# Splitting the decay-gate chain by columns, turning the first q and k in fp32, and more filler matmuls, in a fused attention and SwiGLU kernel

## The chip, the cores and the metric

The kernel runs on one core of one Trainium2 chip. The metric is the time of one execution in microseconds (us) on the device. Runs of one kernel mostly agree within a per cent. Some runs fall in a slower state; they are marked slow and are left out of every comparison below. Where two kernels are compared, they ran on the same chip in alternating rounds. The ratio given is the mean time of one kernel's fast runs over the mean of the other's fast runs in the same rounds, with a 95% interval, so it is not quite the ratio of the medians that are quoted beside it.

A traced run also has a span, from its first to its last instruction. The span is about 1.7 us shorter than the time of the same run.

Names: PE is TensorE's matmul pipe, PEld its loading of the stationary operand, DVE is VectorE, ACT ScalarE, POOL GpSimd, SP SyncE. "SPq" is the DMA issue queue of SyncE.

## The reference

```python
# q, k, v: (8, 8, 576, 64), f: (8, 8, 576), fp32; w_gate, w_val: (512, 1536); w_out: (1536, 512)
scores = q @ k^T / sqrt(64)
cum    = cumsum(log(clip(f, 1e-4, 1)))               # along the sequence
attn   = softmax(causal(scores + cum_i - cum_j))     # per batch and head
x      = (attn @ v) as 4608 tokens x 512
out    = (silu(x @ w_gate) * (x @ w_val)) @ w_out
```

The decay `cum_i - cum_j` is not added to the scores. It is written as four extra rows (a high, a middle and a low part of `cum` in bf16, against rows of ones) under the 64 rows of q and of k. So a score matmul contracts over 68 rows, and the first score needs q, k and these rows.

## The kernel before

All instructions come from a planner. Each piece of work is registered as an `op` with its engine, what it comes after, the buffers it takes and a priority. At build time the planner simulates the engines with guessed durations and emits each operation when it becomes the best one for its engine. Each engine then runs its instructions strictly in that order. What the planner decides is therefore fixed in the program: if one operand comes late on the chip, everything behind it on that engine waits.

The gate chain makes the decay rows of all 64 heads at once, and four ScalarE-issued transfers put those of batches 0 and 1 (`hh` to `QK`) where the score matmuls read them:

```python
o_clip = op(("DVE", ...), ... lf = min(max(lf, 1e-4), 1) ...)
o_ln   = op(("ACT", 0.6), lambda e: nc.scalar.activation(lf, lf, AF.Ln), after=[o_clip], key=-9)
o_scan = op(("DVE", 1.4), ... cum = cumsum(lf), 576 columns at once ..., key=-9)
o_hi   = op(("DVE", 0.7), ... dec[1] = -8 * cum ...)
o_up   = op(("ACT", 0.6), ... dec[0] = 8 * cum ...)
# ... o_r1, o_mid, o_lo: the rest of cum after the bf16 rounding, twice
def row(e, r):
    nc.scalar.dma_start(
        out=QK[D + r : D + r + 1, : FIRST * FB, :, :S].rearrange("o b (j w) s -> o (b j) w s", w=2),
        in_=dec[r][: FIRST * H].rearrange("h w s -> h (w s)"),
    )
```

The queries and keys of a pair of heads are loaded in fp32 as they lie, cast to bf16, turned by six bf16 transposes on TensorE and copied out of PSUM into `QK`:

```python
o1 = op(("SP", SPi), ld_qk, p, nm, bn, ...)                 # load
o2 = op(copier(QT * 2 * D, False), cast_qk, bn, bb, ...)    # fp32 -> bf16, any engine
o3 = op(("PE", mm(*[P] * QT)), turn, bb, bt, ...)           # six transposes
# straighten: two copies out of PSUM, ACT or DVE
```

The weights of the gate products are loaded in four pieces each of `w_gate` and `w_val`, 384 KB a transfer, issued by GpSimd not before a planned time:

```python
w_ready[nm, c] = op(("POOL", SW), weights, t, src, c, key=-3, dma=2.6, ready=W_AT[c] + (nm == "v"))
W_AT = [15.0, 19.0, 36.0, 42.0]
```

While TensorE has nothing to do in the simulated plan, before 22 us, the planner emits filler matmuls. They multiply the identity by itself into an unused bank and only keep TensorE active:

```python
if e == "PE" and idle and idle[0] <= t < idle[1] and self.free["f"]:
    idle[2](self.free["f"][-1])        # dummy(bank)
    busy[e] = t + idle[3]
...
span = plan.run((2.0, IDLE_TO, dummy, 0.2))     # IDLE_TO = 22.0
```

The parts left out are the attention (`score`, `expo`, `mask`, `weigh`, `flip`), the feed-forward part (`gate`, `tanh`, `silu`, `times`, `project`) and the later batches, which the change leaves alone.

The softmax here doesn't subtract the row's maximum and nothing guards it: scores larger than these inputs give would overflow.

## Time and profile before

| | before |
|---|---|
| time, median (four runs) | 410.09 us (409.21 to 515.33, the longest slow) |
| span of the traced run | 407.9 us |
| TensorE busy | 95% of the span |
| first score matmul | 20.97 us |
| first gate matmul | 39.07 us |
| granted clock at half | 14.6 to 35.1 us |

(The prediction read 14.2 to 35.05 us for this stretch; the clock record of the trace has 14.62 to 35.10. The 14.08 us from the first score to 35.05 and their half, 7.04, are kept below: they change by less than 0.1 us.)

The page of the profile cuts the span into 40 equal slices of 10.2 us. A digit is the busy share of a slice in tenths (9 means 90% or more); for PEclk it is the clock that the throttle granted, in tenths of full speed. The DMA row is the mean busy share of the 16 DMA engines. This is the page of the kernel before:

```profile
PE   7399999999999999999999999999999999999995
...
PEclk9757999999999999999999999999999999999999
DMA  9998999249752986979799787975211002002002
```

From the fifth slice on, TensorE is full to the end and its clock is granted. Only the first three or four slices, the head, have anything to give. The timeline of TensorE shows the head closer. A row has the start, the length, the engine and line, the operation with its output and inputs, how many instructions it groups, and in brackets how long TensorE had been idle before it and what ended that. L729 are fillers, L383 transposes, L491 scores, L623 gate matmuls. This is the kernel before, from 11 to 40 us:

```profile
start us, us, engine line op out<-in xcount [idle before <-releaser]
...
13.80 0.60 PE L729 MATMUL ps<-ident 128*128 128x256 bf16 x4 [2.46 <-ACT QK L290]
...
15.16 0.85 PE L383 MATMUL ps<-ident,BF 128*128 128x128 bf16 x6
20.97 0.80 PE L491 MATMUL ps<-QK 68*128 68x256 bf16 x4 [4.96 <-DMA QK<-hh]
...
39.07 0.60 PE L623 MATMUL ps<-xT,wg 128*128 128x256 bf16 x4
```

TensorE stood still for 2.46 us and again for 4.96 us, until the decay rows (`hh`) had landed. The busy times by stretch (microseconds busy and instructions of each engine, then clock, DMA share and GB/s) show what this did to the clock. Kernel before:

```profile
core 0: us, PE busy (x) PEld busy (x) DVE busy (x) ACT busy (x) POOL busy (x), PEclk, DMA share, GB/s
14.00:21.00 7.00, 2.04 (x20) 1.58 (x19) 3.87 (x6) 2.55 (x4) 2.43 (x3) 0.54 1.23 156
21.00:35.00 14.00, 14.00 (x129) 11.46 (x130) 7.07 (x19) 11.12 (x26) 9.14 (x26) 0.50 1.09 207
35.00:50.00 15.00, 13.63 (x181) 11.25 (x180) 12.38 (x27) 13.01 (x30) 10.19 (x26) 1.00 1.08 196
```

From 21 to 35 us TensorE is busy all the time at clock 0.50. In between the DMA share stays above 1: it sums the packets that are under way on each engine, from several queues, so it can exceed 1. The chain of waits (start, length, what) of the kernel before says what the first score hung on:

```profile
10.87 0.76 DVE hh L344
...
13.11 7.72 DMA QK<-hh
...
20.97 0.80 PE ps L491 x4
```

The step of the gate chain in this view (L344, the rounding of the middle part) ends at 11.6 us, the last subtraction (L345) at 12.4 us. The four row transfers were issued from 9.7 to 13.1 us. The last of them took until 20.8 us to land, and the other three had landed only at 18.3 to 18.9 us.

### The profile page before, as it was taken

The page shows a single profiled execution, that of the slowest core. Times are in us where ns is not written, and L with a number is a line of the kernel's source. Part 1 is how long each engine was busy: PE and PEld are TensorE (multiplying, and loading weights), DVE is VectorE, ACT ScalarE, POOL GpSimd, SP SyncE. Part 2 cuts the span into 40 slices and gives each one's busy share as a digit, 9 for nine tenths or more (in the row PEclk, how much of TensorE's full clock was granted, in tenths as well). Part 3 has the DMA queues.
Part 4 walks back from the last instruction along what each step waited for, and adds up shares of the span by engine and source line. Part 5 has one row for each costly group of instructions (what it writes and reads, how often), then busy time and mean ns, then how long its engine had stood idle before and what let it go on. Part 6 is the DMA issues. An engine that isn't in the chain of part 4 may idle for free.

```text
span 407.9 us, 8397 instructions
## 1 busy us (share of the span) xinstructions
PE 388.7 (95%) x3110; PEld 228.8 (56%) x3155; DVE 236.6 (58%) x453; ACT 222.2 (54%) x450; POOL 127.5 (31%) x353
## 2 busy tenths in 40 slices
PE   7399999999999999999999999999999999999995
PEld 4277778745655555555555555556665444444542
DVE  7756888745784287237651775177624861770850
ACT  6378997436853646365655664566677322322321
POOL 7565754504441423234333431433333000000000
PEclk9757999999999999999999999999999999999999
DMA  9998999249752986979799787975211002002002
GB/s 202 200 233 159 208 219 201 53 137 205 144 112 67 196 188 106 140 130 199 107 172 234 139 132 115 233 123 96 55 53 51 2 0 104 2 0 104 1 21 71
DMA packets 103673, 50.11 MB, mean 123 GB/s; under 512 B 87696, under 2 KB 98448, under 8 KB 103312
## 3 DMA queue, kind: packets, MB, share of 16 engines
q1 hardware_dynamic: 97056, 38.65, 46.9%
q0 software_dynamic: 6304, 10.62, 15.8%
q8 instruction: 25, 0.41, 0.4%
q10 hardware_dynamic: 272, 0.30, 0.4%
q14 instruction: 16, 0.13, 0.1%
HBM read 38.34 MB, written 15.78 MB: 133 GB/s over the span
## 4 chain that ended last, share of the span: by engine, by line
PE 90%; DMA 3%; DVE 2%; ACT 2%; issue 1%; DVEq 0%; ACTq 0%
PE ps L623 45%; PE ps L638 23%; PE ps L491 12%; PE ps L522 7%; PE ps L546 2%; DMA QK<-hh 2%; PE ps L383 2%; DVE QK L292 1%; DMA xT<-in_q_dram 1%; ACT QK L290 1%; DVE hh L337 0%; ACT L336 0%; DVE hh L342 0%; ACT PT L499 0%; DVE hh L339 0%
## 5 line engine op out<-in xcount | busy, mean ns | idle before, releaser
L623 PE MATMUL ps<-xT,wv 128*128 128x512 bf16 (+3 forms) x467 | 111.0, 357 | 0.6
L623 PE MATMUL ps<-xT,wg 128*128 128x512 bf16 (+3 forms) x465 | 110.7, 357 | 0.9 <-issue 0.2
L627 ACT ACTIVATE th<-ps 128x512 f32<-128x512 f32 (+3 forms) x120 | 66.6, 555 | 74.7 <-PE ps L623 71.3
L638 PE MATMUL ps<-wo,hh 128*128 128x512 bf16 (+1 forms) x427 | 104.5, 379 | 0.8
L631 DVE SCALAR_TENSOR_TENSOR th<-th,ps 128x512 f32<-128x512 f32 (+3 forms) x120 | 75.5, 629 | 50.4 <-ACT th L627 49.8
L499 ACT ACTIVATE PT<-ps 128x512 bf16<-128x512 f32 (+2 forms) x192 | 92.6, 509 | 19.8 <-PE ps L491 14.5
L634 DVE TENSOR_TENSOR hh<-th,ps 128x512 bf16<-128x512 f32 (+3 forms) x120 | 76.1, 634 | 12.8 <-PE ps L623 0.9
L491 PE MATMUL ps<-QK 68*128 68x320 bf16 (+4 forms) x448 | 76.9, 273 | 5.5 <-DMA QK<-hh 5.0
L508 POOL TENSOR_SCALAR_AFFINE_SELECT PT<-PT 128x128 bf16<-128x128 bf16 (+1 forms) x192 | 53.1, 278 | 90.4 <-ACT PT L499 83.5
L623 PEld LDWEIGHTS <-wg 128*128 128x128 bf16 x480 | 44.8, 97 | 37.3 <-issue 0.4
L638 PEld LDWEIGHTS <-hh 128*128 128x128 bf16 (+1 forms) x444 | 41.7, 98 | 40.7 <-issue 1.2
L623 PEld LDWEIGHTS <-wv 128*128 128x128 bf16 x480 | 44.9, 97 | 34.7
L508 POOL TENSOR_SCALAR_AFFINE_SELECT PTa<-PTa 128x256 bf16<-128x256 bf16 x64 | 26.1, 409 | 87.8 <-ACT PTa L499 86.5
L642 ACT ACTIVATE ot<-ps 128x512 f32<-128x512 f32 (+1 forms) x37 | 22.1, 597 | 49.6 <-PE ps L638 47.9
L522 PEld LDWEIGHTS <-PT 128*128 128x128 bf16 x768 | 39.8, 99 | 15.0 <-POOL PT L508 0.8
L529 DVE RECIPROCAL rc<-ps 128x5 f32<-128x5 f32 (+2 forms) x64 | 12.3, 192 | 61.9 <-PE ps L522 61.6
L522 PE MATMUL ps<-VB,PT 128*128 128x65 bf16 x768 | 47.5, 196 | 0.1
L491 PEld LDWEIGHTS <-QK 68*128 68x128 bf16 x448 | 36.4, 101 | 19.4 <-issue 6.8
L499 ACT ACTIVATE PTa<-ps 128x384 bf16<-128x384 f32 x64 | 31.2, 491 | 20.0 <-PE ps L491 19.9
L292 DVE COPY QK<-ps 64x576 bf16<-64x576 bf16 x27 | 20.2, 753 | 17.1 <-PE ps L383 15.3
L536 DVE TENSOR_TENSOR xn<-ps,rc 128x320 bf16<-128x320 f32 x56 | 27.5, 491 | 1.7
L292 POOL CAST VB<-natv 128x512 bf16<-128x512 f32 (+1 forms) x34 | 20.3, 615 | 2.7 <-DMA natv<-in_v_dram 2.7
(50 smaller groups left out, 185.8 us busy)
## 6 DMA issues: line engine op xcount, KB each, us to landing
out_dram<-ot SPq DMA_DIRECT2D x35, 256.0 KB, 2.3
natv<-in_v_dram SPq DMA_DIRECT2D x32, 256.0 KB, 7.2
xT<-in_q_dram SPq DMA_DIRECT2D x10, 288.0 KB
xT<-in_k_dram SPq DMA_DIRECT2D x10, 288.0 KB, 11.0
qk_d<-in_q_dram POOLq DMA_DIRECT2D x5, 576.0 KB, 6.2
qk_d<-in_k_dram POOLq DMA_DIRECT2D x5, 576.0 KB, 6.9
wg<-in_moe_w_gate_dram POOLq DMA_DIRECT2D x4, 384.0 KB, 8.4
wv<-in_moe_w_val_dram POOLq DMA_DIRECT2D x4, 384.0 KB, 10.8
```

The costliest lines, as they stand in the source:

```text
L292: E[e].tensor_copy(dst, src)
L491: nc.tensor.matmul(s[:, c : c + w], QK[:KR, hqk[p].i, 2 * j + 1, kt * P : (kt + 1) * P], QK[:KR, hqk[p].i, 2 * j, q0 : q0 + w], start=True ...
L499: nc.scalar.activation(place(h, i)[:, OFFS[i] : OFFS[i] + c], ps(bs)[:, :c], AF.Exp, scale=0.125)
L508: nc.gpsimd.affine_select(out=d, in_=d, pattern=pat, compare_op=ALU.is_ge, fill=0.0, base=0, channel_multiplier=-1,)
L522: nc.tensor.matmul(o[:, lo : lo + D + 1], pt[:, c : c + P], VB[hvb[b].i][:, kt, hb, : D + 1], start=first and n == 0, stop=last and n == l ...
L536: nc.vector.tensor_mul(XN[bx.i][:, qb : qb + nq, j], o, r)
L623: nc.tensor.matmul(ps(bf)[:, :n], w[:, ko, fc * P : (fc + 1) * P], xT[:, ko, t0 : t0 + n], start=(ko == 0), stop=(ko == KD - 1))
L627: nc.scalar.activation(TH[bt.i][:, :n], ps(bf)[:, :n], AF.Tanh, scale=0.5)
L631: nc.vector.scalar_tensor_tensor(out=t, in0=t, scalar=1.0, in1=ps(bf)[:, :n], op0=ALU.add, op1=ALU.mult)
L634: nc.vector.tensor_mul(HH[:, bh.i, lo : lo + n], TH[bt.i][:, :n], ps(bf)[:, :n])
L638: nc.tensor.matmul(ps(bf)[:m, :DM], HH[:, hs[fc].i, lo : lo + m], wo[:, fc, :], start=(fc == 0), stop=(fc == KF - 1))
L642: nc.scalar.activation(OT[bo.i][:m], ps(bf)[:m, :DM], AF.Copy, scale=0.5)
```

## The change

The intent is to start the attention earlier and to keep TensorE's clock up on the way:

- The chain is cut into columns 0 to 255 and 256 to 575. The first score blocks need only the first 256 columns, so four small row transfers leave early, on SyncE. The transfers of the second part follow later.
- The q and k of batch 0 are loaded in halves, turned in fp32 without a cast, and cast when they are copied out of PSUM.
- The scratch of the gate chain moves from the hidden buffer `hh` to unused columns of `xT`. So the 432 KB store of the later batches' decay can wait until 45 us.
- Filler matmuls are allowed until 40 us of the simulated plan (22 before); 95 are emitted instead of 39.
- All planned times and priorities are set anew.

```diff
-    o_scan = op(("DVE", 1.4), lambda e: nc.vector.tensor_tensor_scan(
-        out=cum, data0=lf, data1=zero, initial=0.0, op0=ALU.add, op1=ALU.add), after=[o_ln, o_zero], key=-9)
+    CUTS = (slice(0, HALF), slice(HALF, S))
+    def scan(e, c):
+        x = CUTS[c]
+        nc.vector.tensor_tensor_scan(out=cum[:, x], data0=lf[:, x], data1=zero[:, x], op0=ALU.add, op1=ALU.add,
+                                     initial=cum[:, HALF - 1 : HALF] if c else 0.0)
# ... the other steps of the chain likewise, for c in 0, 1
-        nc.scalar.dma_start(                                   # row: four transfers, ACT
+        for p0, p1, x in ((0, FB, CUTS[c]),) if c == 0 else ((0, FB, CUTS[c]), (FB, FIRST * FB, slice(0, S))):
+            E[e].dma_start(                                    # row: four first, eight second, SP
+                out=QK[D + r : D + r + 1, p0:p1, :, x]..., in_=dec[r][2 * p0 : 2 * p1, :, x])
+    def turn_x(e, p, half, xs, bt):
+        ...     nc.tensor.transpose(o, natx[half][p][:, x, h, P * y : P * y + P], ident32[:m, :m])
+    def first_queries(p):
+        for half in range(2):
+            lds = [op(("SP", SPi), ld_x, p, nm, x, half, ...) for x, nm in enumerate("qk")]
+            ...     o3 = op(("PE", ...), turn_x, p, half, xs, bt, ...)
+            ...     straighten_x on ACT or DVE, with the cast
-    queries(0, 0)
-    ...
+    for p in range(FB):
+        first_queries(p)
-    span = plan.run((2.0, IDLE_TO, dummy, 0.2))
+    span = plan.run((2.0, IDLE_TO, dummy, 0.107))
-W_AT = [15.0, 19.0, 36.0, 42.0]
+W_AT = [9.0, 14.5, 11.3, 31.6]
-IDLE_TO = 22.0
+IDLE_TO = 40.0
# ... cuts: the planner's model of DMA queues, buffers, priorities of the other loads
```

## The prediction

> **What bounds the kernel now.** TensorE. In the busy times per stretch it works 301.3 of 303.5 us from 100 us to its last matmul; from 35.05 us on it idles 4.5 us in all. The tail after it is 4.4 us. Only the head can give much. There the chain of waits shows the gate chain, row transfers QK<-hh from 13.11 to 20.83 us, and the first score matmul at 20.97. By microsecond, the granted clock is 1.00 to 14 us, 0.50 from 14.2 to 35.05, then 1.00: matmuls had stopped from 11.3 to 13.8 and 16.0 to 20.97. From 20.97 to 35.05 TensorE is fully busy at 0.50: 14.08 us for 7.04 us of work. The Trainium skill ("TensorE: Matmul & The Clock Gate", Part 1) says that an idle window of about 3.4 us halves the clock and a busy one restores it; here restoring took 14 busy us, so losing the clock costs more than the page suggests.
>
> **What the change does.**
> - The gate chain (scan 1.35, subtract 1.26, 0.75 us) is cut into 256 and 320 columns; the first row sends need only the first part. They stand behind about 2 MB of loads; 0 to 10 us moved 201 GB/s. The 432 KB decay store that competed with the rows moves to much later.
> - Batch 0: eight casts (0.55 to 0.84 us) and 48 bf16 transposes (6 in 0.50 us warm) go; 48 fp32 transposes come. Copies out of PSUM become 24 of 320 to 512 elements (estimate 0.4 to 0.65 us, from the 256- and 512-element ones here) instead of 16 of 0.65 to 0.75. Net relief of the other engines about 5 us, estimate.
> - First weights are asked for at about 9 us instead of 18.5, and gate matmuls stand much earlier in TensorE's order.
> - Fillers 39 -> 95: 62 before the first score, 33 after.
>
> **On the critical path.** First score: 62 fillers (0.22 us cold to about 8 us, 0.11 to 0.14 warm) and six groups of transposes end near 14 us; rows land at about the same time. I put it at 15.2 us (-5.8). Clock kept: -7.0. Against this: at full clock TensorE outruns ScalarE (79% busy from 21 to 35 us with TensorE at half speed) and DMA (share above 1 until 33 us): I expect 6 us idle or filler from first score to 50 us, before 1.4: +4.6. fp32 transposes after first score +1.4 (estimate). Sum -6.8; with the relieved engines -7.7.
>
> **Prediction: 402.5 us, range 396.5 to 408.5.** Chances: faster by over 2% 0.46, within 2% 0.50, slower 0.04.
>
> **Signs.** Right: first score matmul at 14 to 17 us; granted clock 1.00 from 9 us on; first gate matmul before 30 us instead of 39; last matmul about 7 us earlier; the length from 100 us on unchanged; ScalarE over 90% busy from 16 to 45 us. Wrong: clock back at 0.50 after the first score; row sends landing after 18 us; TensorE idle over 8 us between first score and 50 us, released by weights (DMA) or ScalarE.
>
> **What would make it wrong.** Slower: the attention matmuls (68 rows, 65 columns) may count as too little activity, since 14 busy us did not raise the clock; then 7 us come back. Row sends sharing with weight loads may land late, fillers run out, and the gap drops the clock. Fillers placed for a guessed timeline may delay real work. Faster: if gate matmuls fill TensorE after the first score, the gain approaches 11 us (about 399).

## The result, and the profile after

| | before | after |
|---|---|---|
| time, median (four runs each, the longest of each slow) | 410.09 us (409.21 to 515.33) | 406.67 us (406.17 to 412.7) |
| ratio of fast runs | | 0.992 [0.9896, 0.9944] |
| span of the traced run | 407.9 us | 404.4 us |
| first score matmul | 20.97 us | 14.92 us |
| first gate matmul | 39.07 us | 28.92 us |
| last matmul ends | 403.53 us | 400.46 us |
| granted clock at half | 14.6 to 35.1 us | 24.6 to 31.4 us |

The change is worth 3.4 us where 7.7 us were forecast; the time lies within the range. The page of the changed kernel:

```profile
PE   8969999999999999999999999999999999999996
...
PEclk9979999999999999999999999999999999999999
DMA  8999999047953985899699789986102002002002
```

The third slice has still lost clock. The timeline of TensorE in the changed kernel from 14 us on (L813 fillers, L580 scores, L485 fp32 transposes, L635 flips, L712 gate matmuls):

```profile
13.83 1.25 PE L813 MATMUL ps<-ident 128*128 128x256 bf16 x10
14.92 1.32 PE L580 MATMUL ps<-QK 68*128 68x256 bf16 x14
...
22.27 0.50 PE L485 MATMUL ps<-ident,xT 80*128 80x80 f32 x4 [1.95 <-DMA xT<-in_k_dram]
...
24.39 2.03 PE L580 MATMUL ps<-QK 68*128 68x192 bf16 x10 [0.99 <-DMA QK<-xT]
...
27.17 0.74 PE L485 MATMUL ps<-ident,xT 80*128 80x80 f32 x4
28.09 0.77 PE L485 MATMUL ps<-ident,xT 80*128 80x80 f32 x4 [0.17 <-DMA xT<-in_k_dram]
...
28.92 1.06 PE L712 MATMUL ps<-xT,wg 128*128 128x256 bf16 x4
```

The first score starts at 14.92 us as intended. Then TensorE waits for two things that it had not waited for before: at 22.27 us for the second half of pair 2's k, at 24.39 us for the rows of the second part. The busy times by stretch show the new loss of clock, in 25 to 30 us, and a DMA share of 1.14 to 1.37 all through. Changed kernel:

```profile
14.00:20.00 6.00, 5.77 (x75) 4.96 (x74) 2.76 (x9) 4.19 (x10) 5.56 (x13) 1.00 1.24 242
20.00:25.00 5.00, 2.07 (x25) 1.53 (x22) 1.58 (x6) 1.96 (x6) 2.85 (x5) 0.96 1.37 199
25.00:30.00 5.00, 4.80 (x26) 3.33 (x25) 1.31 (x3) 3.06 (x7) 0.82 (x3) 0.50 1.23 234
30.00:35.00 5.00, 4.93 (x44) 4.07 (x44) 2.53 (x6) 4.55 (x12) 3.81 (x13) 0.86 1.14 210
```

The chain of waits of the changed kernel at this place consists of loads alone, until the last turn at 28.09 us:

```profile
13.61 8.62 DMA xT<-in_k_dram
...
22.24 5.71 DMA xT<-in_k_dram
...
28.09 0.78 PE ps L485 x4
```

The issue queue of SyncE in the changed kernel shows how they line up. L352 are row transfers, about 0.68 us each; L473 are halves of q and k:

```profile
13.61 0.44 SPq L473 DMA_DIRECT2D xT<-in_k_dram  x1
14.14 5.88 SPq L352 DMA_DIRECT2D QK<-xT  x6
20.07 0.44 SPq L473 DMA_DIRECT2D xT<-in_q_dram  x1
22.24 0.32 SPq L473 DMA_DIRECT2D xT<-in_k_dram  x1
```

The trace also shows why one load follows from another in the chain. SyncE gives each transfer the semaphore of the eighth before it and waits until that one has landed. The k half issued at 22.24 us has the semaphore of the k half issued at 13.61, whose last landing is at 22.22 us.

Beside them GpSimd issues the six weight transfers (changed kernel, GpSimd's timeline, the first and the last of the six):

```profile
9.52 0.99 POOL L708 DMA_DIRECT2D wg<-in_moe_w_gate_dram  x1
...
15.88 0.79 POOL L708 DMA_DIRECT2D wv<-in_moe_w_val_dram  x1
```

The account, worked out from the two traces, after minus before: first score -6.05; clock -3.8 (7.04 us lost before; 3.3 after, half of the 6.56 us that TensorE was busy from 24.58 to 31.41); fillers after the first score +3.5 (33 of 0.107 us); TensorE idle from first score to 50 us +2.1 (3.4 against 1.4); more transposing after the first score +1.0; tail -0.4. The sum is -3.7 and the span's change is -3.5. Such an account adds terms as if they were independent, and the experiments show that they are not.

### The profile page after: what moved, and what is told of

It is laid out like the page before. It is cut to its first block, busy times and chain, and to the rows that moved or that the text cites. A ratio compares the mean times of both kernels' runs of the same rounds, so it can differ in the third digit from the quotient of the medians.

```text
span 404.4 us, 8602 instructions
## 1 busy us (share of the span) xinstructions
PE 394.4 (98%) x3211; PEld 232.3 (57%) x3211; DVE 230.6 (57%) x452; ACT 224.9 (56%) x457; POOL 128.9 (32%) x357
## 4 chain that ended last, share of the span: by engine, by line
PE 91%; DMA 4%; DVE 1%; POOL 1%; ACT 1%; issue 0%; SPq 0%; ACTq 0%; DVEq 0%
PE ps L712 46%; PE ps L727 24%; PE ps L580 10%; PE ps L611 7%; DMA xT<-in_k_dram 4%; PE ps L635 2%; PE ps L418 1%; DMA xT<-in_f_dram 1%; PE ps L813 0%; DVE xT L321 0%; POOL PT L380 0%; DVE QK L297 0%; POOL xT L328 0%; POOL wg L708 0%; SPq L352 0%
## 5 line engine op out<-in xcount | busy, mean ns | idle before, releaser
L712 PE MATMUL ps<-xT,wg 128*128 128x512 bf16 (+3 forms) x480 | 113.7, 359 | 0.0
L712 PE MATMUL ps<-xT,wv 128*128 128x512 bf16 (+3 forms) x480 | 113.4, 358 | 0.1
L727 PE MATMUL ps<-wo,hh 128*128 128x512 bf16 (+1 forms) x444 | 106.3, 379 | 0.0
L588 ACT ACTIVATE PT<-ps 128x384 bf16<-128x384 f32 (+2 forms) x192 | 93.0, 507 | 23.8 <-PE ps L580 14.0
L580 PE MATMUL ps<-QK 68*128 68x320 bf16 (+4 forms) x448 | 72.9, 265 | 1.1 <-DMA QK<-xT 1.0
L712 PEld LDWEIGHTS <-wv 128*128 128x128 bf16 x480 | 45.0, 98 | 35.5 <-issue 0.4
L712 PEld LDWEIGHTS <-wg 128*128 128x128 bf16 x480 | 45.1, 98 | 35.3
L611 PEld LDWEIGHTS <-PT 128*128 128x128 bf16 x768 | 38.3, 97 | 17.7 <-POOL PT L597 1.1
L611 PE MATMUL ps<-VB,PT 128*128 128x65 bf16 x768 | 45.4, 193 | 0.0
L580 PEld LDWEIGHTS <-QK 68*128 68x128 bf16 x448 | 35.1, 98 | 11.8 <-issue 1.7
L588 ACT ACTIVATE PTa<-ps 128x384 bf16<-128x384 f32 x64 | 30.7, 491 | 15.4 <-PE ps L580 15.2
L295 ACT ACTIVATE QK<-ps 64x576 bf16<-64x576 bf16 (+2 forms) x31 | 19.3, 627 | 9.9 <-DVE QK L297 8.1
L297 POOL CAST VB<-natv 128x512 bf16<-128x512 f32 (+1 forms) x38 | 23.2, 620 | 4.6 <-DMA natv<-in_v_dram 4.6
```

Of the source, the lines that this page charges most:

```text
L297: E[e].tensor_copy(dst, src)
L580: nc.tensor.matmul(s[:, c : c + w], QK[:KR, hqk[p].i, 2 * j + 1, kt * P : (kt + 1) * P], QK[:KR, hqk[p].i, 2 * j, q0 : q0 + w], start=True ...
L588: nc.scalar.activation(place(h, i)[:, OFFS[i] : OFFS[i] + c], ps(bs)[:, :c], AF.Exp, scale=0.125)
L611: nc.tensor.matmul(o[:, lo : lo + D + 1], pt[:, c : c + P], VB[hvb[b].i][:, kt, hb, : D + 1], start=first and n == 0, stop=last and n == l ...
L712: nc.tensor.matmul(ps(bf)[:, :n], w[:, ko, fc * P : (fc + 1) * P], xT[:, ko, t0 : t0 + n], start=(ko == 0), stop=(ko == KD - 1))
L727: nc.tensor.matmul(ps(bf)[:m, :DM], HH[:, hs[fc].i, lo : lo + m], wo[:, fc, :], start=(fc == 0), stop=(fc == KF - 1))
```

## The experiments

All but two of the experiments (`w_none` and `whole`) edit what the planner has emitted, its order, its fillers or the queue of a transfer, and nothing else. The planner's emissions are recorded as a list `log` of (operation, engine), with `None` for a filler and its bank; the list is edited and then emitted. By its code, a list without an edit emits the kernel it came from; no run checks this, but the trace of `w_late`, which only moves transfers, has as many instructions as that of the changed kernel (8602). `at(tag)` is the place of an operation in the list. All results were correct except where said. Medians are of six runs, the kernel before's of eleven in the same rounds. The changed kernel's own median of 406.67 us comes from other rounds, so small differences to it are read from traces, and differences of medians under about 1 us are not relied on.

Two marks are read from the traces: the first gate matmul, and the first matmul of the output projection (called first projection below), before which every one of these kernels has issued the same 192 gate matmuls. From the first projection to the last matmul the time is nearly fixed: 329.27 us in the changed kernel, 329.27 in `fill_gap`, 329.25 in `no_post_fill`, 329.26 in `w_at_20`; 327.18 in the kernel before, 327.18 in `before_fill`, 327.19 in `before_fill_store_late`. So in these traces what moves the first projection arrives at the end. Between the two kernels even this mark needs care: the changed one reaches it 5.17 us earlier (71.18 against 76.35 us), but leaves 15 score matmuls and 15 of the products with v for later, and takes 2.09 us longer from there.

Theory A, of the prediction: the clock that fell again and the fillers are the missing 4 us. Theory D: the order of SyncE's queue delays what TensorE waits for. Theory A1: the weight transfers take the DMA engines from the loads. Theory E: the head up to the first gate is bound by what the DMA engines move altogether, so that what TensorE gains there is waited away, while from the first gate on TensorE passes on any delay to the end. Rival R: the end is set elsewhere.

### Holding the clock through the gap

```diff
+ n = at(("turnx", 2, 1), 1);  log[n:n] = [(None, 1)] * 18     # before the late transposes
+ n = at(("s", 0, 1));         log[n:n] = [(None, 3)] * 9      # before the second-part scores
```

> The changed kernel with 27 fillers added where its trace shows TensorE waiting on transfers: 18 before the transposes that started at 22.27 us, 9 before the second-part scores that started at 24.39 us. Nothing else moves. Theory A (the gaps of 1.95 and 0.99 us let the clock fall at 24.8 us, and 6.4 us at half speed cost 3.2 us): the granted clock stays 1.00 after 14 us, and the time falls by about 3 us, to about 403.5 us, for the fillers stand in waits and cost nothing. Rival C (the activity of the attention matmuls is too low, whatever stands in the gaps): the clock falls to 0.50 near 25 us again and the time stays within 0.7 us of 406.6. If the fillers outlast the waits, up to 1 us is lost.

Measured: 407.1 us, ratio to before 0.9945 [0.9921, 0.9968], traced span 404.8 us. The clock stayed at 1.00 until 29.7 us (mean 0.97 from 25 to 30 us, 0.50 in the changed kernel) and was then at half for 3.41 us instead of 6.83. Nothing was gained: TensorE reached pair 3 earlier and waited for its halves instead. Timeline of TensorE with the gap filled:

```profile
27.70 0.47 PE L485 MATMUL ps<-ident,xT 80*128 80x80 f32 x4 [0.64 <-DMA xT<-in_k_dram]
...
28.15 0.60 PE L712 MATMUL ps<-xT,wg 128*128 128x256 bf16 x4
```

The first gate comes at 28.15 instead of 28.92 us. But the half-clock stretch, 29.71 to 33.12 us, now lies behind it, and the first projection comes at 71.59 instead of 71.18 us. So holding the clock up to the first gate was worth 0.77 us there: the rest of the loss lay in the shadow of these transfers. Theory A's mechanism (the gap drops the clock) held.

The run doesn't test a clock that stays full behind the first gate too, as A had expected. From the first gate to the first projection `gate_late` (below), at full clock, needs 41.42 us; the changed kernel, with 2.49 us at half clock, 42.26; this run, with 3.41 us at half clock, 43.44. An estimate from these numbers puts the first projection of a changed kernel with a full clock throughout at 28.15 + 41.42 = 69.57 us at best, 1.6 us earlier than it was. That is about half of what A expected, and no run shows it.

### Removing the fillers after the first score

```diff
+ n = at(("s", 0, 0));  log[n:] = [x for x in log[n:] if x[0] is not None]
```

> The changed kernel without the 33 fillers that stand after the first score matmul. My ledger counts 3.5 us for them. If they cost that: the 15 of them after 31 us give back 1.6 us, and the 18 before 24 us nothing, because TensorE then waits for transfers anyway: about 405 us if the clock falls no earlier. Rival (the fillers after the first score hold the clock): the clock falls before 22 us instead of at 24.8 and stays down longer, time 407 to 412 us.

Measured: 406.52 us, ratio 0.9942 [0.9917, 0.9967], traced span 404.4 us. The clock fell earlier (mean 0.71 from 20 to 25 us), and the first gate came at 29.02 us. The first projection came at 71.18 us in both. The 33 fillers neither cost nor help; their +3.5 us in the account was time in which TensorE would have waited or run at half clock (10.24 us of it here, 6.83 in the changed kernel).

### Fillers in the kernel before, without the rest of the change

```diff
+ n = ...  log[n:n] = [(None, 3)] * 23      # in the gap at 11.3 us
+ n = at(("s", 0, 0));  log[n:n] = [(None, 0)] * 46
```

> The kernel before with 69 fillers added in its two gaps (23 after 11.3 us, 46 before the first score at 20.97 us) and nothing else changed. It measures the clock term of the prediction by itself. My prediction's arithmetic: the clock stays 1.00, 7.0 us come back, and up to 4.6 us of that is lost again to ScalarE and DMA, which gives 403 to 408 us with the first score still at about 21 us. If keeping the clock is worth its full 7 us: 403. If TensorE at full clock only waits for the other engines: 408 to 410. Rival C (attention matmuls have too little activity to hold the clock): the clock falls again within 8 us of the first score, and the time is within 1.5 us of 410.

Measured: 406.25 us, ratio 0.9937 [0.991, 0.9965], traced span 403.9 us, mean clock of the whole run 1.000. The first score comes at 21.53 us, 0.56 later than before, and the first gate at 35.38 us instead of 39.07. This is the changed kernel's gain from two short lists of fillers, without the early rows and the fp32 turning. Timeline of TensorE in that kernel:

```profile
21.53 0.49 PE L491 MATMUL ps<-QK 68*128 68x256 bf16 x4 [0.96 <-DMA QK<-hh]
...
35.38 0.60 PE L623 MATMUL ps<-xT,wg 128*128 128x256 bf16 x4
```

The busy times of that kernel:

```profile
14.00:21.50 7.50, 6.56 (x65) 5.71 (x65) 4.00 (x6) 2.69 (x4) 2.44 (x4) 1.00 1.20 160
21.50:35.00 13.50, 12.33 (x190) 9.76 (x190) 10.85 (x26) 13.11 (x33) 10.43 (x30) 1.00 1.21 241
```

From 21.5 to 35 us TensorE runs at full clock, and ScalarE is busy for 13.11 of 13.50 us. The attention matmuls that ran at half clock from 21 to 35 us in the kernel before hold the full clock here, so rival C of the expectation falls. In the old order, too, the full clock is not worth the 7.04 us that half the pulses of 14.08 us amount to. From the first score to the first gate it took 18.10 us before and 13.85 here, 4.25 less. That ScalarE sets the rate then is argued from its busy share of 97% and not tested; TensorE itself counts as busy for 12.33 of the 13.50 us.

### A later start of the scores

```diff
+ n = at(("s", 0, 0));  log[n:n] = [(None, 3)] * 28
```

> The changed kernel with 28 fillers (3.0 us at full clock) added directly before the first score matmul, which then starts near 17.9 us instead of 14.9. Theory D (until 28 us TensorE waits for transfers anyway, so the early start is off the critical path): the time stays within 0.8 us of 406.6. If the early start does pay: about 409.5 us.

Measured: 407.29 us, ratio 0.9951 [0.9923, 0.9979], traced span 406.3 us. The first score started at 18.02 us instead of 14.92, the second-part scores at 24.48 instead of 24.39, the last turn at 28.39 instead of 28.09 and the first gate at 29.22 instead of 28.92. Its timeline at the first gate:

```profile
29.22 1.06 PE L712 MATMUL ps<-xT,wg 128*128 128x256 bf16 x4
```

Of 3.1 us given away, 0.3 reached the first gate, and 0.35 the first projection (71.53 us). (The traced span holds another 1.37 us of a wait at 248 us, of which more below.) So nearly 3 of the 6 us gained at the first score are off the critical path.

### Reordering SyncE's queue, with and without later weights

```diff
+ n = first second-part row transfer in log
+ log[n:n] = [k half of pair 2, q and k halves of pair 3]     # moved from later places
  # loads_first_w_late: also the gate weights c2 and c1 after mask(7, 0), at about 20 us
```

> The changed kernel with only the order of the SyncE queue changed: the second half of k of pair 2 and the second halves of q and k of pair 3 are issued before the second row sends instead of between and after them. New theory D: in the changed kernel the pair-3 halves are issued at 20.1 and 22.2 us, because each of six row sends takes about 0.7 us of the queue and a load waits for the eighth before it; they land near 28 us, and TensorE, which takes its instructions in order, cannot start the first gate matmul before that, so the six microseconds won at the first score are lost again. D expects the pair-3 halves to land before 23 us, the first gate matmul at 24 to 26 us instead of 28.9, and 403 to 405.5 us. Rival A1 (the weight transfers' share of the DMA engines sets the landing, whatever the order): the pair-3 halves land after 25 us or the row sends slip as far, and the time stays within 0.8 us of 406.6.

> The order of the run before this one, and the second and third pair of gate weights issued at about 20 us, after the eighth mask. If order and contention both matter, the halves and the rows all land by 21 us, the clock stays 1.00 and the time is 401 to 404.5 us. If contention does not matter once the order is right (D alone): equal to the run with only the order, within 0.8 us. If the late weights then hold up gate matmuls: slower than that run by 1 us or more.

Measured: 410.36 us, ratio 1.0024 [0.9988, 1.0059], for the first (its traced run is slow, so its trace is not used) and 410.57 us, 1.003 [1.0016, 1.0045], for the second, with a span of 408.8 us. In the second, the k half of pair 2 was turned at 20.87 us instead of 22.27. But the rows, now behind the loads, were late instead:

```profile
28.17 2.19 PE L580 MATMUL ps<-QK 68*128 68x192 bf16 x10 [6.16 <-DMA QK<-xT]
...
32.44 1.06 PE L712 MATMUL ps<-xT,wg 128*128 128x256 bf16 x4
```

TensorE waited 6.16 us for them. The order in the queue decides who is late, but a better order than the planner's was not found here. Theory D explains which wait ends last, not that there is one.

### Later weights: four of six, all six, and spread

```diff
  # w_late: weights c2, c1 moved after mask(7, 0)
  # w_at_20: all six
+ late = [log.pop(at(("w", nm, c))) for c in (0, 2, 1) for nm in "gv"]
+ n = at(("mask", 7, 0)) + 1;  log[n:n] = late
  # w_mid: c0 before mask(0, 0), c2 after mask(4, 0), c1 after mask(7, 0)
```

> The changed kernel with the second and third pair of gate-weight transfers issued after the eighth mask (about 20 us) instead of at 12.6 to 15.9 us; nothing else moves. Theory A1 (the second halves of k and the second rows landed late, at 22.2 and 24.4 us, because the weight queue took the larger share of the DMA engines): they land at least 2 us earlier, the gap before 22.27 us shrinks below 0.7 us, the clock stays 1.00 and the time falls by 2 to 5 us, to 402 to 405, unless gate matmuls then wait for the later weights. Rival B (the order and the eight outstanding transfers of the SyncE queue set the landing): landings and gap stay where they were, and the time is equal or longer.

> The changed kernel with all six early gate-weight transfers issued after the eighth mask (near 20 us) instead of from 9.5 us on; nothing else moves. A clean test of contention (A1) for what lands before 20 us. If the weights' traffic delays the second halves and the second rows: k of pair 2 lands before 19 us instead of 22.3, the last rows before 21.5 instead of 24.4, and the wait of 1.95 us before 22.27 us is gone. If it does not (D: the SyncE queue sets it): both stay within 1 us of 22.3 and 24.4. In either case the first gate matmul waits for its weights until 27 to 31 us and the time is 406 to 410 us; this run is for the landings.

> The changed kernel with the six weight transfers spread between the two schedules tried: the first pair issued at about 13 us (9.5 in the changed kernel), the second at about 18.5, the third at about 20.5. Theory E: the attention loads land earlier than in the changed kernel (last turn of pair 3 at about 26 against 28.1), the first weights arrive before the first gate is ready, at about 27 us; time 405.5 to 407. If the sum of the bytes alone decides and their order cannot: first gate again at 28 to 29 and time 406.5 to 408.5. Rival R: 406 to 407 whatever the order.

`w_late`: 408.28 us, ratio 1.0002 [0.9962, 1.0043]. The second-part scores came 1.5 us earlier (22.88 us), the last turn at 27.91 and the first gate at 28.74, hardly earlier. But the clock was at half from 23.86 to 37.51 us, 8.77 us of it behind the first gate, and the first projection came at 74.86 instead of 71.18 us (0.85 us of this was a wait for a cast of v). Behind the first gate a lost clock does cost.

`w_at_20`: 409.76 us, ratio 1.0013 [0.9987, 1.0039], traced span 407.6 us. The weights were issued from 21.3 to 26.0 us. The busy times of its first two stretches:

```profile
14.00:20.00 6.00, 5.90 (x74) 5.35 (x72) 2.65 (x7) 3.19 (x9) 2.31 (x6) 1.00 0.23 53
20.00:25.00 5.00, 4.69 (x53) 3.66 (x53) 2.67 (x9) 4.79 (x12) 4.47 (x7) 1.00 1.11 220
```

Without the weights the DMA engines are busy 0.23 instead of 1.24 from 14 to 20 us and move 53 instead of 242 GB/s. And no load keeps TensorE waiting any more. Its timeline:

```profile
24.37 0.72 PE L485 MATMUL ps<-ident,xT 80*128 80x80 f32 x8
25.03 0.30 PE L580 MATMUL ps<-QK 68*128 68x320 bf16 x1
28.22 1.03 PE L712 MATMUL ps<-xT,wg 128*128 128x256 bf16 x4 [2.90 <-DMA wg<-in_moe_w_gate_dram]
31.30 1.03 PE L712 MATMUL ps<-xT,wv 128*128 128x256 bf16 x4 [2.05 <-DMA wv<-in_moe_w_val_dram]
```

The last turns come at 24.37 and the last score of this part at 25.03 us, 3.6 us earlier than in the changed kernel (28.65). Then TensorE waits for the weights, 2.90 and 2.05 us, and the second gate group starts at 31.30 instead of 30.07 us. So A1 is right about the traffic: the 2.3 MB of weights are what made the halves and the rows late. But the weights are needed themselves, right behind.

`w_mid` tried an order between the two: 408.59 us, ratio 0.999 [0.9969, 1.0011]. The first gate came at 26.82 us, 2.1 us earlier than in the changed kernel. Then the next load was late, a block of v. Its timeline:

```profile
26.82 0.60 PE L712 MATMUL ps<-xT,wg 128*128 128x256 bf16 x4
...
32.35 0.31 PE L611 MATMUL ps<-VB,PT 128*128 128x65 bf16 x5 [2.29 <-POOL VB L297]
```

The first projection was 0.8 us later (71.97 us), although the clock was full all along. That is theory E in one trace: attention loads and first weights came earlier, and v paid for it. Its traced run also lost time much later, to which I come back.

### The rows on ScalarE's queue

```diff
+ log = [(o, "ACT") if o is the transfer of a second-part row else (o, e) for o, e in log]
```

> The changed kernel with the eight second row sends issued by ScalarE's queue, in the same places of the order, instead of SyncE's; SyncE then issues the halves of pairs 1 to 3 without a row send between them. D (queue time of SyncE is the limit): the halves of pair 3 are issued before 16 us instead of 20.1 and 22.2, land before 24 us, first gate matmul before 27 us, 404 to 406 us. A1 (the DMA engines are full): they are issued earlier but land at 26 us or later, and the time is within 0.8 us of 406.6, or longer if ScalarE's exponentials wait behind the sends.

Measured: 408.67 us, ratio 0.996 [0.9924, 0.9997], traced span 406.5 us. This takes the row transfers out of SyncE's queue, and TensorE waits for no load before the first gate. But ScalarE now spends about 0.7 us on each of eight issues, which it also had to wait to make (2.17 us for three, 2.19 for two), and its exponentials come late. Timeline of TensorE:

```profile
18.39 0.33 PE L580 MATMUL ps<-QK 68*128 68x256 bf16 x2 [1.69 <-ACT PTa L588]
...
21.00 0.59 PE L813 MATMUL ps<-ident 128*128 128x256 bf16 x2 [0.91 <-ACT PTa L588]
```

The first gate came at 29.30 us. The wait moved from a DMA to ScalarE.

### No weight transfers at all

```diff
- nc.gpsimd.dma_start(out=t[:, :, lo:hi], in_=src[:, :, lo:hi])     # pieces c0, c1, c2
+ nc.gpsimd.memset(t[:, :, lo:hi], 0.03125)
```

> The changed kernel, but the six early transfers of gate weights (384 KB each, 2.3 MB) are not made: a memset of a constant on GpSimd fills each piece instead. The result is wrong on purpose. It measures what these transfers cost the head and whether an earlier head is worth anything to the whole. Theory E (the head is bound by what the 16 DMA engines move, the weights included; an earlier head shortens the whole): second half of pair 2 by 20.5 us, last scores and first gate by 25.5 us with no wait for a DMA, clock full through the head, and the time 402.5 to 404.5 us, that is 2 to 4 us below the changed kernel's 406.7. Rival R (the time is set behind the head, by the other engines and by later transfers, so that the head's end is in a shadow as well): first gate also near 25.5 us, but the time stays at 406 to 407.

Its output is wrong, which doesn't matter for the time. Measured: 406.66 us (404.0 to 409.82), ratio 0.9932 [0.9895, 0.997], traced span 402.9 us. There was no wait for a DMA in the head and the clock stayed at 1.00. But the memsets stood before the masks on GpSimd, and TensorE waited 2.15 us for a mask, so the first gate came at 27.47 us and not at the 25.5 that every theory expected. The traced run is 1.5 us shorter than the changed kernel's, as the first gate is 1.45 us earlier; the median is not. By its time this run fits rival R and misses what E expected; by its trace it fits E. It does not decide.

### A later first gate

```diff
+ n = at(("gp", 0, 0));  log[n:n] = [(None, bank of this gate)] * 28
```

> The changed kernel with 28 filler matmuls (3.0 us at full clock) put directly before the first gate matmul and nothing else changed. Three of the earlier runs moved the first score by 3 us, the clock and the fillers, and the time did not move; this one delays the point that those had left where it was. Theory E (everything up to the first gate is in the shadow of transfers, and from the first gate on the rest of the kernel hangs on TensorE): first gate at 32 to 33 us, some of the half-clock stretch saved because the fillers keep TensorE busy, the first projection (71.2 us in the changed kernel) 2 to 3 us later, the time 408.5 to 409.7. Rival R (the rest of the kernel has slack that takes up what the head gains or loses): first gate as late, but the time within 0.7 us of the changed kernel's, 406 to 407.4.

Measured: 410.56 us (409.8 to 415.48), ratio 1.0044 [1.0, 1.0088], traced span 411.3 us. The fillers and the first gate in its timeline:

```profile
28.52 4.44 PE L813 MATMUL ps<-ident 128*128 128x256 bf16 x28
32.80 0.60 PE L712 MATMUL ps<-xT,wg 128*128 128x256 bf16 x4
```

The first gate is 3.9 us later than in the changed kernel, the first projection 3.0 us later (74.2 instead of 71.2 us), and the median 3.9 us higher than 406.67. The 3.0 us are what the trace shows to be passed on; the rest of the median's difference can be the later stall described below, which this trace has. Twenty-eight fillers put before the first score cost nearly nothing up to the first gate; the same twenty-eight put before the first gate arrive at the end. Rival R, which expected at most 407.4, falls. (The median is a microsecond above E's own interval, 408.5 to 409.7. The delay at the first gate was itself 0.9 us above the 3 us of the fillers, since much of them ran at half clock.)

### A later decay store in the kernel before

```diff
+ the fillers of before_fill, 23 and 14 of them
+ store = log.pop(...);  log.insert(after the first loads of batch 1, store)
```

> The kernel before with fillers in its gaps (23 after 11.3 us, 14 before the first score) and the 432 KB store of the decay rows issued after the first loads of batch 1 instead of ahead of the last row send. It gives the old kernel both things that the change was for, a warm clock and an early first score, without fp32 transposes or split transfers. Expected: the rows land near 16 to 17 us, first score at 16 to 18 us instead of 21.5, clock 1.00. If an early start pays when all of batch 0's q and k are already there: 402 to 404.5 us, against 406.25 with the fillers alone. If the early start is worth nothing there either (weights and ScalarE bound the stretch to 45 us): 405.5 to 407.

Measured: 410.63 us, ratio 1.0028 [1.0015, 1.0041], traced span 409.0 us. The rows did not land earlier; the first score started at 22.79 us after a wait of 5.69 us for them. As I had planned fewer fillers, the clock fell. So the store was not what made the rows slow in the kernel before. The loads of v ahead of them are a candidate (in this run the DMA share is 1.40 at only 106 GB/s from 15 to 20 us), but no run takes them away, and this stays open.

### The change without the fp32 turning

```diff
-     first_queries(p)
+     queries(p, (0, 5, 10, 20)[p])       # batch 0 as in the kernel before: loaded whole, cast, turned in bf16
```

> The change without its fp32 half turning: batch 0's q and k are loaded whole first, cast to bf16 and turned as before the change; the split gate chain, the early first rows, the scratch in x, the weight times and the fillers stay, and the planner orders the rest anew. If what held TensorE from 15 to 28 us is that half of q and k was put off behind rows and weights (D or A1): all four pairs are in QK before the first score, that starts at 17 to 20 us, TensorE idles less than 3 us from then to 50 us, and the time is 402 to 405 us, below both kernels. If the half turning was worth its early start: 407 to 410 us.

Measured: 416.9 us, ratio 1.0209 [1.017, 1.0249], traced span 414.0 us. Here the planner had to plan anew, so other things moved too; the edit itself also moves four memsets from GpSimd to VectorE and changes the buffers into which two later pairs are loaded. The first score came at 21.29 us, about where it was in the kernel before. TensorE then waited 4.02 us for a cast of v whose load landed at 29.9 us, and from 50 to 60 us worked only 6.54 of 10 us, with four waits of 0.4 to 2.0 us for an exponential, a cast and copies. The run shows that the early rows alone do not give the early score and that the new order needs the half loads. It doesn't isolate the fp32 turning, since its priorities were tuned for another order.

### A stall that comes and goes

In the traces of five fast runs TensorE waits near 248 to 252 us for decay rows of a later pair, for 1.37 us (`start_late`), 1.99 (`w_late`), 2.04 (`gate_late`), 2.13 (`rows_on_act`) and 4.44 us (`w_mid`):

```profile
251.99 0.56 PE L580 MATMUL ps<-QK 68*128 68x256 bf16 x4 [4.44 <-DMA QK<-dec_d]
```

In the traces of the changed kernel, `fill_gap`, `no_post_fill`, `w_at_20`, `w_none` and `loads_first_w_late` it is missing. It belongs to none of the edits, and the traced spans that hold it are too long by it (and by the half clock that follows: 0.83 from 250 to 260 us in `w_mid`). It is one source of the spread of these kernels. What brings it about was not tried.

## Why the prediction was right or wrong

- **First score 15.2 us, -5.8: right in size (14.92, -6.05), wrong in worth.** `start_late` gave 3.1 us of it away and lost 0.3 at the first gate. From 14.92 to 28.1 us TensorE does only about 6 us of useful work (busy 9.84 us, less 1.9 of filler and an estimated 1.7 for the half clock). The prediction treated the time of the first score as a point from which everything follows; it isn't, when the loads behind it are spread over 13 us.
- **"Clock kept: -7.0" is the step that failed.** The clock fell again, from 24.6 to 31.4 us, so that the account has -3.8 for it; of the 4.0 us between the forecast's -7.7 and the account's -3.7, this term is 3.2. The text had named this danger ("the gap drops the clock"), but for the rows of the first score; it came 10 us later from k halves and second-part rows. And the term was too big even where the clock is kept: `before_fill` keeps it throughout and its span is only 4.0 us shorter and its median 3.4 us lower than the kernel before's of the same rounds, with ScalarE busy for 97% of the stretch. Nor did holding it up to the first gate of the changed kernel shorten the whole (`fill_gap`): transfers set the pace up to there, and the half clock then came behind it. Half of a half-clock stretch is an upper bound, which I booked as a gain.
- **Idle and filler +4.6: mis-sized.** It measured +5.6 (2.1 idle, 3.5 filler). The two are one thing, time before the next load, as `no_post_fill` shows. The prediction listed idle, early start and clock as separate terms and summed them. They trade against each other up to the first gate, so their sum has no meaning there.
- **What limits the head: named only in part.** The prediction saw the DMA share above 1 and weights asked for at 9 us. It drew the danger for the first rows and not for what came after. `w_at_20` shows that the weights are what the halves and rows wait behind; `w_at_20`, `w_mid` and the reordered queues show that moving them moves the wait to weights, v or rows. `gate_late` shows that a delay of the first gate is passed on. An earlier first gate is not passed on by itself: in `fill_gap` it came 0.8 us and in `w_mid` 2.1 us earlier, and the first projection 0.4 and 0.8 us later.
- **fp32 transposes +1.4: about right (+1.0).** The -0.9 for relieved engines has no counterpart that could be shown.
- **Signs.** First gate before 30 us: right (28.92). Clock 1.00 from 9 us on: wrong. Row sends landing after 18 us, a sign of wrong: the first-part rows had landed at 13.7 us, the second-part rows of batch 0 landed from 19.1 to 24.1 us. ScalarE over 90% busy from 16 to 45 us: wrong in the changed kernel (21.36 of 29 us, 74%) and in `before_fill` (23.27 of 29, 80%). Last matmul about 7 us earlier: it was 3.1. TensorE idle over 8 us from first score to 50 us, a sign of wrong, did not come (3.4).

Shown: the early score has slack, the fillers of the changed kernel and all but 0.8 us of its clock loss before the first gate lie in the shadow of transfers, fillers alone give the old kernel the same time, a delay of the first gate is passed on. Argued and not shown: that ScalarE limits the old kernel with fillers; that no order of these transfers could do better, since only a handful were tried. Not tested: the changed kernel's own order with a full clock behind the first gate as well. A kernel that beats both was not found; the old one with fillers (406.25) and the changed one (406.67) are alike within their spread.

Two statements of the Trainium skill bear on this. "TensorE: Matmul & The Clock Gate", Part 1, says that an idle window of about 3.4 us halves the clock and a busy one of that length restores it. These traces agree on the length: a half-clock stretch between two full ones lasts 3.41 us or a multiple of it (6.83, 10.24, 13.65, 20.48 us). But no idle window was needed to lose the clock: in the 3.41 us before it fell, TensorE had been busy for 39% of the time in the changed kernel and for 54% in `fill_gap`. And restoring it took longer than one window, 14 us from the first score before and 6.8 us after; in `fill_gap` and `start_late` it was back after 3.41 us. "DMA: Bandwidth & Descriptors", section "Issuing engines are not separate DMA queues", says that transfers issued by SyncE, ScalarE and GpSimd run on the same 16 DMA engines and interleave. `w_at_20` agrees: taking GpSimd's weights away let the last turn, which needs SyncE's last half, start 3.7 us earlier (24.37 against 28.09 us).

## What to carry to other kernels

Before adding up gains in a stretch, look for the point where it next waits for something that the change doesn't speed up, and count only what moves that point; delaying it on purpose by a known amount, and delaying an earlier point by the same, is a cheap way to find it. Try the cheapest part of a change alone: here some 70 filler matmuls in the old kernel were worth as much as the whole rewrite. When a head needs all its loads anyway, issuing one class earlier makes another late, and removing one class for a test run shows which.

## What the Trainium skill lacked or had wrong

- "TensorE: Matmul & The Clock Gate", Part 1, gives about 3.4 us of busy time for the clock to come back. In these runs matmuls of attention (68 rows contracted, 65 to 320 columns), back to back, ran at half clock for 14 us (21 to 35 us, TensorE busy 14.00 of 14.00) in the kernel before. In the changed one it took 6.83 us, with fp32 turns and gate matmuls among them. In `before_fill` the same attention matmuls held a full clock from 21.5 to 35 us. Of transposes, Part 4 of the page says that they don't count as busy in the same way; what these attention matmuls count for, it doesn't say.
- The same page, "Terms", takes the penalty of throttled time as that time times the share of pulses withheld. For the stretch of 14.08 us that is 7.04 us; keeping the clock was worth 4.25 us between the same two instructions and 4.0 us at the end, with ScalarE busy for 13.11 of 13.50 us. Here the formula is an upper bound, and the page doesn't say so.
- "DMA: Bandwidth & Descriptors", "Issuing engines are not separate DMA queues", calls the issue time that a second issuing engine saves usually small. One row's 0.68 us is small beside the 5.5 us that it took to land (issued at 18.63, landed at 24.14 us in the changed kernel). But they add up: six rows held SyncE for 4.1 us of issue, 5.88 with the waits between, before the next q half; on ScalarE three took 2.17 and two 2.19 us, waits included, and held up the exponentials (TensorE waited 1.69 and 0.91 us for them).
- No page read says how long small row transfers within SBUF take while the DMA engines are loaded: the one issued at 13.11 us landed at 20.83 us in the kernel before, and the last second-part row of batch 0, issued at 18.63, landed at 24.14 us in the changed one and let the scores start at 24.39.
